# Gated attention, then hash-routed experts: identity products at the start, the multiplication by u a step later, the last group's turns in one piece, the last small block at the very end

## The chip, the cores and the metric

One NeuronCore of a Trainium2 chip runs the whole program. The metric is the device time of one execution in microseconds; the kernel before was run three times: 2505.44, 2507.41 and 2507.57, median 2507.41 us.

The engines by the names that the profile uses: PE is TensorE (matrix products; PEld its weight loads), DVE VectorE, ACT ScalarE, POOL GpSimd, SP SyncE, which here only issues DMAs. A "q" behind a name means the engine's queue that issues DMAs.

## The reference

```python
# attention: u, v are (8, 2496, 256), z is (8, 2496, 64), all float32
scores = (1.0 / S) * np.matmul(z, z.transpose(0, 2, 1))
attn = np.maximum(scores, 0.0) ** 2
x = u * np.matmul(attn, v)              # then reshaped to (19968, 256)
# experts: w1 is (8, 256, 1024), w2 is (8, 1024, 256)
expert_idx = token_ids * np.int64(2654435761) % np.int64(E)
for e in range(E):
    mask = expert_idx == e
    h = np.maximum(x[mask] @ w1[e], 0.0)
    out[mask] = h @ w2[e]
```

The score matrix is symmetric, and each token goes to exactly one expert, which its token id alone decides.

## The kernel before, in words

**Attention.** Each of the 8 batches is cut into 5 groups of queries (two stretches of up to 256, one of each half of the sequence) and 5 groups of keys. A step is one (batch, query group, key group), 200 in all, in the list `steps`; five steps with the same query group follow each other, and `pos` counts them 0 to 4. For a step, `score` (L212) makes the products of z (L228, tile `s_ps`) and ScalarE and VectorE turn them into squared positive scores `a` (L242 to L250). Scores below the diagonal are not computed: `mirror` (L267) transposes a finished tile, `keep` stores it in DRAM, and `recall` (L287) loads it back. `sums` (L256) forms four combinations `t` of the score quarters, `add_v` (L189) three of v, and `attend` (L297) multiplies in seven products instead of eight, a Strassen-like scheme, each of them accumulated over the five steps in half of a PSUM tile `acc` (L310). Four such tiles exist, and one group takes all four. After the fifth step `join` (L313) reads the seven sums and combines them into the output quarters `o`: ScalarE copies the first, VectorE does L322 to L328. The next group's first product overwrites what L322 reads, so it can only start behind it.

The main loop, from L773, runs ahead: in step i the scores and sums of step i + 2 are prepared, then `attend` of step i, then `join` at `pos` 4. The group's output is transposed on VectorE (`gate`, L331) and written to DRAM at `pos` 1 of the next group (`put`). At `pos` 3 `fetch` (L353) reads it back with tokens on partitions, as `x_row`, together with the rows of u (`u_sb`, L206). Five steps later, again at `pos` 3 and at the end of the step, `multiply` (L370, its operation on L374) multiplies `x_row` by u: four operations on VectorE. In this and the next step GpSimd scatters the rows to the slots of their tokens' experts (`sort`, L395, `x_slots` in DRAM).

While attention runs, `places` computes on VectorE and GpSimd which slot each token gets, `prepare` makes weight blocks with the sums that the seven-product scheme needs, and `enter` writes the token number of each slot.

**The last group** (batch 7, group 4) has no time for the way through DRAM. `gate_late` (L376) turns its output on TensorE instead (`transpose`, L384, into the PSUM tile `g_ps`), multiplies by u on VectorE (L386) and scatters. It is a generator that is advanced between parts of the first expert block. The group before it is fetched two steps before the end and multiplied at the end of the last step.

**Experts.** Sorted tokens are processed in 32 large blocks of 512 tokens and 35 small ones of 128. `load_x` reads rows from `x_slots`, `turn_x` transposes them on VectorE; for the first two blocks this is done inside the last two steps of attention (`turn_x_at_once`). `up_large` and `down_large` (L886, L917) make seven products each per part, in the order 1, 6, 7, 5, 2, 3, 4 that `products` (L860) writes out: VectorE's L866 adds the first two sums, L871, L872, L879 and L882 the rest, and `store` (L854, GpSimd) scatters finished rows to the output, four stores for a large block, one for a small. Products 1 and 5 go to PSUM tiles with the tag "held", in which later products are added; 6, 7 and 4 take tiles with the tag "other", of which `down_large` has one. `up_small` and `down_small` (L946, L962) are the plain two products of a small block.

The order of the work on TensorE is written out by hand in `ORDER` (L976): each letter advances one generator by a part. U and D are the large block's first and second product, u and d the small block's, X and x the transposition of rows for the next blocks, and G the generator `gate_late`. In the last round (i = 32) only D and d are left.

Of the kernel before, what the change touches and what calls it, by code (L numbers as in the profile page):

```python
# [11 lines left out]
F32 = mybir.dt.float32  # L12
# [13 lines left out]
def kernel(  # L26
# [10 lines left out]
    nc = tc.nc  # L37

    B, S, D = u.shape
    K = z.shape[-1]  # L40
    N = B * S
    E, _, F = moe_w1.shape
# [3 lines left out]
    P = 128  # L46
    L = 32
    DP = D // P
# [6 lines left out]
    NL = -(-(N - E * (BLK - 1)) // BLK)  # L55
# [9 lines left out]
    NT = -(-HS // (2 * P))  # L65
# [68 lines left out]
    ident = const.tile([P, P], F32)  # L134
# [8 lines left out]
    def keys(s, j):  # L143
        return P if (s, j) != (NT - 1, 1) else KL
# [225 lines left out]
    def multiply(b, g, x_sb):  # L370
        for q in range(2):
            for t in range(2):
                x, y = times_u(b, g, x_sb, q, t, keys(g, t))
                nc.vector.tensor_mul(x, x, y)  # L374

    def gate_late(b, g, o):  # L376

        x_sb = late.tile([P, 2, 2, D], F32, name="x_row")
        for q in range(2):
            ps = down_ps.tile([P, 2, D], F32, name="g_ps", tag="any")  # L380
            for t in range(2):
                m = keys(g, t)
                for i in range(DP):
                    nc.tensor.transpose(ps[0:m, t, ts(i, P)], o[:, i, q, ds(t * P, m)], ident[:])  # L384
                x, y = times_u(b, g, x_sb, q, t, m)
                nc.vector.tensor_mul(x, ps[0:m, t].rearrange("p (h i k) -> p i h k", h=DP, k=L), y)  # L386
                sort(b, g, x_sb, 2 * q + t)
            yield

    def sort(b, g, x_sb, k):  # L390

# [14 lines left out]
    SURE = 2  # L406
# [301 lines left out]
    def turn_x_at_once(j):  # L708
        for _ in turn_x(j):
            pass  # L710
# [17 lines left out]
    order = tc.manual_schedule()  # L728
    order.__enter__()

    for c in range(NZ):
        load_z(0, c, (nc.sync, nc.scalar) if c < 2 else None)
        if c < 2:
            turn_z(0, c)
        if c == 1:
            load_v(0, 0)
# [36 lines left out]
    for i, (b, g, s) in enumerate(steps):  # L773
# [11 lines left out]
        if pos == 0:  # L785
            acc = [acc_ps.tile([P, 2, W], F32, name="acc", tag="acc") for _ in range(4)]
        attend(b, g, s, ready.pop(i), acc, pos == 0, pos == NT - 1)
        if i >= len(steps) - SURE:
            turn_x_at_once(i - len(steps) + SURE)
        if pos == NT - 1:  # L790
            done = (b, g, join(g, acc, opool if i < len(steps) - 1 else late))
        prepare_mirror(i + AHEAD, a)
# [22 lines left out]
        if i >= 5 and not is_routed:  # L815
            is_routed = next(routed, True) is True
            if is_routed:

                rowpool = attention.enter_context(tc.tile_pool(name="rowpool", bufs=2))
        elif is_routed:  # L820
            if fetched and i >= fetched[0][0] + (5 if i < len(steps) - NT else 2):
                rows = fetched.pop(0)[1]
                multiply(*rows)
                to_sort += [(*rows, k) for k in range(4)]
            for _ in range(min(2, len(to_sort))):
                sort(*to_sort.pop(0))
            if len(fetched) < 2 and waiting and (len(waiting) > 1 or i > put_at + (1 if i < len(steps) - NT else 0)):
                fetched.append((i, fetch(*waiting.pop(0))))
# [133 lines left out]
    def down_small(j):  # L962
        ps = down_ps.tile([P, D], F32, name="o_ps", tag="any")
        for f in range(FP):
# [10 lines left out]

    ORDER = {"": "UuUDUuUDUdUDU" "XUDXUDUxUDUUDU", "made": "UuUDUuUDUdUDU" "XUDXuUDUxuUDUUDU",  # L976
             "next": "UuUDUuUDUdUDU" "XUDXUDUxUDUUxDU", "last": "UdUDUuUDUuUDU" "XUDXUDdUxUDUUDU",
             "first": "UUUUGUUGUUUUUUUU", "second": "DUDUUDUUDUUDUU" "xXUuDUXUuDUxUU"}

# [3 lines left out]
    def at(i):  # L985

        return [i, *SMALL[i]] if 0 <= i < NL else []

    for i in range(NL + 1):
# [10 lines left out]
        if i == 1:  # L1000
            parts["x"].insert(0, turn_x(SMALL[1][0]))
        parts = {p: chain(*x) for p, x in parts.items()}
        for p in ORDER["first" if i == 0 else "second" if i == 1 else next((k for k, n in (("made", i), ("next", i + 1), ("last", i - 1)) if len(at(n)) > 2), "")]:
            next(parts.get(p, iter(())), None)
        for p in parts.values():
            assert next(p, None) is None and next(p, "end") == "end"
# [45 lines left out]
```

## Time and profile before

The profiled execution took 2507.8 us; its span, from the first to the last instruction, is 2506.0 us, and the mean granted TensorE clock 0.998 of full speed.

| stage (us from the start) | length | PE busy | PE idle | DVE busy | share of DMA engines |
|---|---|---|---|---|---|
| 0 to 17.25: before the first product with v | 17.25 | 8.85 | 8.40 | 6.53 | 1.02 |
| 17.25 to 1453.9: the rest of attention | 1436.65 | 1430.68 | 5.97 | 1094.29 | 0.83 |
| 1453.9 to 1476: first expert block, last group's turns | 22.10 | 15.31 | 6.79 | 14.61 | 0.91 |
| 1476 to 2497.9: the experts | 1021.90 | 1021.54 | 0.36 | 537.52 | 0.68 |
| 2497.9 to 2506: behind the last product | 8.10 | 0 | 8.10 | 0.42 | 0.18 |

PE idle is length less PE busy. A share of the DMA engines above 1 means that transfers overlap on an engine. In the timeline's lines the columns are: start and duration in us, engine, line, operation, output<-inputs with shape, count of instructions merged into the row, and in brackets the idle time of the engine before it and what ended it. A line of the waits reads: engine, tile and line that waited <- what it waited for: us in total, times, longest. A line of the stretch tables: stretch, its length, busy time of the engine asked for, granted clock, DMA share, GB/s.

### The profile page before, as it was taken

How to read it: one execution, taken by the hardware profiler on the slowest of the kernel's cores; microseconds unless marked ns; L12 is line 12 of the kernel's file. 1: busy time of each engine (PE TensorE's matmuls, PEld its weight loads, DVE VectorE, ACT ScalarE, POOL GpSimd, SP SyncE). 2: the span in 40 equal slices, each digit the busy share in tenths (PEclk: the TensorE clock that was granted, in tenths of full speed). 3: DMA queues.
4: the chain of work that ended last, by engine and by line, in shares of the span. 5: the costliest groups of instructions: out<-in, count | busy, mean ns of one | idle time of the engine just before them, and what ended most of it. 6: DMA issues, size and time to landing. Idle time of an engine off the chain costs nothing.

```text
span 2506.0 us, 36968 instructions
## 1 busy us (share of the span) xinstructions
PE 2476.4 (99%) x13631; PEld 2110.9 (84%) x13631; DVE 1653.4 (66%) x3151; ACT 705.8 (28%) x1203; POOL 548.9 (22%) x532
## 2 busy tenths in 40 slices
PE   8999999999999999999999989999999999999998
PEld 6787787787787777877787889999999999999998
DVE  7798768768778677687687665545555555555553
ACT  4324324224223233133233112222222222222221
POOL 0000333322332233233223221111111111111112
PEclk9999999999999999999999999999999999999999
DMA  8776899798797897897888797766676667667762
GB/s 148 201 206 176 244 272 227 211 248 203 234 262 191 244 249 184 251 250 198 246 244 230 200 284 240 244 227 227 236 236 203 222 225 232 204 224 245 236 217 72
DMA packets 604661, 557.19 MB, mean 222 GB/s; under 512 B 287068, under 2 KB 544685, under 8 KB 594240
## 3 DMA queue, kind: packets, MB, share of 16 engines
q1 hardware_dynamic: 513984, 369.74, 54.6%
q10 hardware_dynamic: 63168, 97.86, 11.9%
q0 software_dynamic: 27328, 87.23, 10.0%
q8 instruction: 107, 1.75, 0.3%
q14 instruction: 74, 0.61, 0.1%
HBM read 375.55 MB, written 175.60 MB: 220 GB/s over the span
## 4 chain that ended last, share of the span: by engine, by line
PE 91%; DMA 5%; DVE 2%; issue 1%; SPq 0%; ACT 0%; POOL 0%; POOLq 0%; DVEq 0%; ACTq 0%
PE acc L310 42%; PE o_ps L931 16%; PE h_ps L901 15%; PE s_ps L228 8%; PE h_ps L954 5%; PE o_ps L965 5%; DMA a<-scores 3%; DMA u_sb<-in_u_dram 1%; DMA scores<-mirror 0%; DMA zn<-in_z_dram 0%; DVE x_row L374 0%; DVE t L261 0%; DVE t L262 0%; DVE t L263 0%; ACT a L242 0%
## 5 line engine op out<-in xcount | busy, mean ns | idle before, releaser
L242 ACT ACTIVATE a<-s_ps 128x512 f32<-128x512 f32 (+2 forms) x508 | 248.1, 579 | 736.5 <-PE s_ps L228 697.5
L310 PE MATMUL acc<-t,vc 128*128 128x256 f32 (+3 forms) x1600 | 402.6, 374 | 0.0
L310 PEld LDWEIGHTS acc<-a,v_sb 128*128 128x128 f32 (+1 forms) x1600 | 293.3, 190 | 125.0 <-issue 45.5
L310 PE MATMUL acc<-a,v_sb 128*128 128x256 f32 (+3 forms) x1600 | 382.6, 382 | 5.3 <-DVE o L322 5.2
L395 POOL DMA_INDIRECT x_slots<-x_row,row x160 | 192.3, 1202 | 849.7 <-DVE x_row L374 642.9
L310 PE MATMUL acc<-t,v_sb 128*128 128x256 f32 (+3 forms) x1600 | 369.7, 373 | 0.0
L310 PEld LDWEIGHTS acc<-t,vc 128*128 128x128 f32 (+1 forms) x1600 | 303.0, 190 | 34.5
L310 PEld LDWEIGHTS acc<-t,v_sb 128*128 128x128 f32 (+1 forms) x1600 | 303.5, 190 | 33.6
L261 DVE TENSOR_TENSOR t<-a 128x512 f32<-128x512 f32 (+1 forms) x200 | 134.5, 672 | 226.5 <-ACT a L250 162.0
L901 PE MATMUL h_ps<-xs,w 128*128 128x256 f32 x1024 | 258.1, 380 | 0.0
L931 PEld LDWEIGHTS o_ps<-w,h 128*128 128x128 f32 x2048 | 248.6, 192 | 6.5
L228 PE MATMUL s_ps<-zT 64*128 64x512 f32 (+1 forms) x960 | 241.4, 617 | 9.1 <-DVE zT L171 8.4
L931 PE MATMUL o_ps<-w,h 128*128 128x128 f32 x2048 | 249.3, 275 | 0.0
L908 ACT ACTIVATE h<-h 128x512 f32<-128x512 f32 x192 | 121.0, 630 | 349.1 <-DVE h L872 153.2
L854 POOL DMA_INDIRECT out_dram<-o_sb,idx x128 | 126.7, 990 | 420.8 <-ACT h L908 271.2
L272 DVE STREAM_TRANSPOSE mirror<-a 128x512 f32<-128x512 f32 x320 | 198.4, 677 | 6.6 <-DMA scores<-mirror 6.5
L310 PE MATMUL acc<-a,vc 128*128 128x256 f32 (+3 forms) x800 | 201.1, 374 | 0.0
L901 PE MATMUL h_ps<-xT,w 128*128 128x256 f32 x768 | 194.0, 382 | 1.2 <-DVE h L872 1.2
L901 PEld LDWEIGHTS h_ps<-xs,w 128*128 128x128 f32 x1024 | 178.5, 191 | 15.5
L931 PEld LDWEIGHTS o_ps<-w,hs 128*128 128x128 f32 x1536 | 186.4, 192 | 4.8
L931 PE MATMUL o_ps<-w,hs 128*128 128x128 f32 x1536 | 187.1, 275 | 0.0
L611 POOL DMA_INDIRECT slot_tokens<-token,addr x160 | 169.7, 1061 | 49.0 <-issue 48.1
(154 smaller groups left out, 2756.7 us busy)
## 6 DMA issues: line engine op xcount, KB each, us to landing
w<-w_blocks SPq DMA_DIRECT2D x64, 1792.0 KB, 11.3
scores<-mirror SPq DMA_DIRECT2D x276, 256.0 KB, 4.8
a<-scores ACTq DMA_DIRECT2D x48, 1024.0 KB, 5.8
w1s<-in_moe_w_dram SPq DMA_DIRECT2D x35, 1024.0 KB, 10.3
w2s<-in_moe_w_dram SPq DMA_DIRECT2D x35, 1024.0 KB, 11.5
a<-scores ACTq DMA_DIRECT2D x32, 896.0 KB, 7.3
w_blocks<-w POOLq DMA_DIRECT2D x16, 1792.0 KB, 8.1
u_sb<-in_u_dram SPq DMA_DIRECT2D x72, 256.0 KB, 5.2
```

Of the source, the lines that this page charges most:

```text
L228: nc.tensor.matmul(to, z_h[:, ds(h * HS + s * W + j * P, P)], at, start=True, stop=True)
L242: nc.scalar.activation(to, at, AF.Relu, scale=1.0 / S)
L261: nc.vector.tensor_sub(t1, y12, y11)
L272: nc.vector.transpose(m[:, :, j, h].rearrange("p (n i) k -> p i n k", i=QB), a[:, j, h].rearrange("p (i t) q r -> p i (t q) r", t=2))
L310: nc.tensor.matmul(acc[k][:, half, 0:w], x[0:n, j, :], y[0:n, j], start=(first and j == 0 and half == 0), stop=(last and j == 1), skip_gro ...
L395: st = nc.gpsimd.indirect_dma_start(out=x_dram[:, :], out_offset=bass.IndirectOffsetOnAxis(ap=row[0:m, c:c + 1], axis=0), in_=x_sb[0:m, q, ...
L611: st = nc.gpsimd.indirect_dma_start(out=slot_dram[:, None], out_offset=bass.IndirectOffsetOnAxis(ap=addr[0:n, to:to + 1], axis=0), in_=tok ...
L854: st = nc.gpsimd.indirect_dma_start(out=out[:], out_offset=bass.IndirectOffsetOnAxis(ap=idx[:, col:col + 1], axis=0), in_=o, in_offset=Non ...
L901: nc.tensor.matmul(ps[:, r], w1[j][:, k, ts(f + r, P)], y, start=first and r == 0, stop=True, skip_group_check=True)
L931: nc.tensor.matmul(ps[:, t], x[:, f, ts(t, P)], w2_block(w2[j], k)[:, f], start=first and t == 0 and f == 0, stop=f == FQ - 1, skip_group_ ...
L954: nc.tensor.matmul(ps[:, i, :], w1[j][:, c, ts(f + i, P)], x[:, 0, c, 0:P], start=(c == 0), stop=(c == DP - 1))
L965: nc.tensor.matmul(ps[:], hid[j][:, f], w2[j][:, f, :], start=(f == 0), stop=(f == FP - 1))
```

## The change

It has four parts.

- Twelve products of the identity with itself, into a PSUM tile of the score products' pool, are issued first on TensorE; nothing reads them.
- `multiply` comes six steps after `fetch` in place of five until the last ten steps of attention, five in the next five of them and two in the last five, as before; with six it falls at `pos` 4, behind `join`. For the last group but one it moves from the end of the last step to a place ahead of the last `join`. `turn_x_at_once` for the first two blocks runs one step earlier each.
- `gate_late` makes all eight transposes, into two tiles with the tag "held", in its first part, and all four multiplications and scatters in its second. In the first round's order the first G comes after four U's, as before, and the second after three more.
- In the last round the order is `DDDDDDDd`: all seven products of the large block, then the small block's. Before, the d stood between the second and the third D.

```diff
     def gate_late(b, g, o):
 
         x_sb = late.tile([P, 2, 2, D], F32, name="x_row")
+        made = []
         for q in range(2):
-            ps = down_ps.tile([P, 2, D], F32, name="g_ps", tag="any")
+            made.append(down_ps.tile([P, 2, D], F32, name="g_ps", tag="held", bufs=2))
+            for t in range(2):
+                for i in range(DP):
+                    nc.tensor.transpose(made[q][0:keys(g, t), t, ts(i, P)], o[:, i, q, ds(t * P, keys(g, t))], ident[:])
+        yield
+        for q in range(2):
             for t in range(2):
                 m = keys(g, t)
-                for i in range(DP):
-                    nc.tensor.transpose(ps[0:m, t, ts(i, P)], o[:, i, q, ds(t * P, m)], ident[:])
                 x, y = times_u(b, g, x_sb, q, t, m)
-                nc.vector.tensor_mul(x, ps[0:m, t].rearrange("p (h i k) -> p i h k", h=DP, k=L), y)
+                nc.vector.tensor_mul(x, made[q][0:m, t].rearrange("p (h i k) -> p i h k", h=DP, k=L), y)
                 sort(b, g, x_sb, 2 * q + t)
-            yield
+        yield
...
+    warm = mm_ps.tile([P, P], F32, name="warm", tag="mm")
+    for _ in range(12):
+        nc.tensor.matmul(warm[:], ident[:], ident[:], start=True, stop=True)
...
         attend(b, g, s, ready.pop(i), acc, pos == 0, pos == NT - 1)
-        if i >= len(steps) - SURE:
-            turn_x_at_once(i - len(steps) + SURE)
+        if 0 <= i - (len(steps) - 3) < SURE:
+            turn_x_at_once(i - (len(steps) - 3))
+        if i == len(steps) - 1:
+            multiply(*fetched[0][1])
         if pos == NT - 1:
             done = (b, g, join(g, acc, opool if i < len(steps) - 1 else late))
...
-            if fetched and i >= fetched[0][0] + (5 if i < len(steps) - NT else 2):
+            if fetched and i >= fetched[0][0] + (6 if i < len(steps) - 2 * NT else 5 if i < len(steps) - NT else 2):
                 rows = fetched.pop(0)[1]
-                multiply(*rows)
+                if i < len(steps) - 1:
+                    multiply(*rows)
                 to_sort += [(*rows, k) for k in range(4)]
...
-             "first": "UUUUGUUGUUUUUUUU", "second": "DUDUUDUUDUUDUU" "xXUuDUXUuDUxUU"}
+             "first": "UUUUGUUUGUUUUUUU", "end": "DDDDDDDd", "second": "DUDUUDUUDUUDUU" "xXUuDUXUuDUxUU"}
...
-        for p in ORDER["first" if i == 0 else "second" if i == 1 else next((k for k, n in (("made", i), ("next", i + 1), ("last", i - 1)) if len(at(n)) > 2), "")]:
+        for p in ORDER["first" if i == 0 else "second" if i == 1 else "end" if i == NL else next((k for k, n in (("made", i), ("next", i + 1), ("last", i - 1)) if len(at(n)) > 2), "")]:
```

## The prediction

> **What bounds the kernel now.** I read the busy table first, then TensorE's own waits, then its idle time cut by stage, and only then the timeline at each idle place.
>
> ```profile
> PE 2476.4 (99%) x13631; PEld 2110.9 (84%) x13631; DVE 1653.4 (66%) x3151; ACT 705.8 (28%) x1203; POOL 548.9 (22%) x532
> PE s_ps L228 <- DVE zT L171: 8.4, 2, 7.3
> PE g_ps L384 <- DVE x_row L386: 5.6, 2, 4.7
> PE acc L310 <- DVE o L322: 5.2, 7, 1.9
> ```
>
> TensorE (PE) is busy 2476.4 of 2506.0 us, so no reordering can gain more than the 29.6 us it is idle, unless its clock rises. Cut by stage, that idle time is 8.4 us up to 17.25 us, 6.0 in the rest of attention, 6.8 between 1453.9 and 1476, 0.4 in the experts and 8.1 after the last product. The change has one edit for each of the four large pieces.
>
> **Start: identity products.** Twelve 128x128 products of the identity are issued first on TensorE.
>
> ```profile
> 7.26 6.08 PE L228 MATMUL s_ps<-zT 64*128 64x512 f32 x16 [7.26 <-DVE zT L171]
> 13.38 1.77 DVE L171 STREAM_TRANSPOSE zT<-zn 128x736 f32<-128x736 f32 x2
> 14.47 2.78 PE L228 MATMUL s_ps<-zT 64*128 64x512 f32 x8 [1.14 <-DVE zT L171]
> ```
>
> A score product leaves two records here. Later four of them (eight records) take 1.92 us on the chain of waits, 0.48 each; here the pairs begin at 8.27, 9.12 and 9.98 us, 0.855 apart. So the array starts at nearly half speed although the granted-clock column prints 1.00, and four records take 1.92 us from 9.98 but 1.05 from 12.28: by then it is at full pace. The identity is ready at 1.38 us. An expert product of the same 128x128 shape leaves two records of 0.112 us pitch (sixteen L931 records, starts 1.79 us apart), so twelve last 2.7 us at full pace and 4.8 to 5.4 at the slow one: they end by 6.9, before 7.26, and can delay nothing. At full pace the first four score products end at 9.3 instead of 11.04; ScalarE's two pairs (1.08 us each) end at 10.6 instead of 12.16; the square L246 behind them (1.23) ends at 11.8 instead of 13.42; the third turn of z follows it. The fourth turn needs the last z transfer, issued at 9.49 and landing 3.2 to 4.0 us later, so 12.7 to 13.5. I take 13.0, plus 0.9 for the turn: 13.9 instead of 15.15. **Term 1.2 us**; 0 if the array is still slow at 7.26, 1.6 if the transfer is not last.
>
> The Trainium skill, page "TensorE: Matmul & The Clock Gate", Part 1, says the gate opens only after a free-running window of about 3.4 us was busy, and may shut after an idle one. The trace agrees as far as it goes: slow from 7.26 until some time between 10.8 and 12.3. By the page alone, a burst of about 5 us need not contain a whole window, so the term would be 0 or 1.2 at about even chance, an estimate from its window; the trace lets the gate open 3.6 to 5.0 us after the start, and I keep 1.2.
>
> **Attention: u a step later.** The four multiplications by u (L374, 1.43 us together) stand on VectorE ahead of the join of the group; the next group's products wait for the join's first read of the sums (L322).
>
> ```profile
> 884.63 1.66 DVE L374 TENSOR_TENSOR x_row<-x_row,u_sb 128x256 f32<-128x256 f32 x4 [1.84 <-DMA u_sb<-in_u_dram]
> 888.47 0.42 DVE L322 TENSOR_TENSOR o<-r,acc 128x256 f32<-128x256 f32 x1
> 888.94 1.78 PE L310 MATMUL acc<-a,v_sb 128*128 128x224 f32 x8 [0.89 <-DVE o L322]
> ```
>
> TensorE's timeline at the same place (third row) shows 0.89 us idle, released by L322. The other such gaps are 1.92 (at 379), 0.45 (560), 0.69 (707), 0.58 (741), 0.42 (1068) and 0.20 (1248). After the change the multiplication follows the join in VectorE's order, about 8 us later, one step. The same work stands in front of everything after it, and less in front of the join: at least 1.33 us, and 3.1 where u was late. Six gaps vanish (3.2 us); the one at 379 shrinks from 1.92 to 0.59. **Term 4.6 us**, from 3.2 (that one unchanged) to 5.2 (all). What waits for the multiplication is GpSimd's scatter L395 and, behind it in the same queue, the loads of weights L633 and the slot entries; GpSimd waits 642.9 us in 34 waits for x_row as it is, 19 each, with 22% of its time busy. The next fetch that needs a freed buffer of u comes four steps, 32 us, later. SyncE's order changes only in the first two batches. Moving `turn_x_at_once` a step forward changes no order on VectorE, since nothing else lies between: 0 both ways.
>
> **Transition: turns together.** Before, the third and fourth turns wait for VectorE to read the first two; the six rows show who is late.
>
> ```profile
> 1457.17 0.36 PEld L384 LDWEIGHTS g_ps<-ident,o 128*128 128x128 f32 x2
> 1457.74 0.43 DVE L374 TENSOR_TENSOR x_row<-x_row,u_sb 128x256 f32<-128x256 f32 x1 [0.56 <-DMA u_sb<-in_u_dram]
> 1458.81 1.10 DVE L374 TENSOR_TENSOR x_row<-x_row,u_sb 128x256 f32<-128x256 f32 x3 [0.64 <-DMA u_sb<-in_u_dram]
> 1462.48 0.51 PE L384 MATMUL g_ps<-ident,o 128*96 128x128 f32 x2 [4.71 <-DVE x_row L386]
> 1464.00:1466.00 2.00, 0.50 1.07 442
> 1474.21 1.13 PE L901 MATMUL h_ps<-xT,w 128*128 128x256 f32 x4 [1.18 <-DVE h L872]
> ```
>
> (The fifth is SyncE's stretch table: the granted clock was 0.50.) The change puts the multiplications of group 3 ahead of the last join. They wait for the same transfers of u, landing at 1457.7 and 1458.8, while the join used to run from 1454.64 to 1457.18. Now it runs from 1459.9 to 1462.4, and all eight turns wait for it: TensorE, done with its four first products at 1457.5, stands idle 4.9 us instead of 4.7 + 0.9. Then VectorE decides. At full clock: three additions 0.69 each to 64.5, product 3 to 65.4, product 4 to 66.3, L882 to 67.2, four multiplications (1.43) to 68.6, four sums (2.6) to 71.2, L866, L871, L872 to 73.4: TensorE resumes at 1473.45 instead of 1474.21, +0.76. If the clock drops again as it did, TensorE gives product 3 one microsecond later and it resumes at 1474.5, -0.3. **Term 0.2 us.** If u landed before the join were due, the join would end at 1458.7 and the same sum ends at 1470.0: +4.2. If u lands 2 us later, -2. The last scatters come some 3 us later (four at 1.28 after 67.5 or more, against the last at 1468.93); behind them on SyncE wait w1s L720 (1472.15), then the row loads xqs and xq (1472.92 to 1479.6), wanted by VectorE at 1493.6. With 8.6 us of landing xq is there at 1486, so 3 us are covered; beyond 7 they show.
>
> **End: the small block last.**
>
> ```profile
> 2485.33 3.62 PE L965 MATMUL o_ps<-w2s,h 128*128 128x256 f32 x16
> 2485.60 0.42 DVE L866 TENSOR_TENSOR ro<-ro,o_ps 128x256 f32<-128x256 f32 x1 [0.56 <-PE o_ps L931]
> 2501.15 0.97 POOL L854 DMA_INDIRECT out_dram<-o_sb,idx  x1 [0.30 <-issue]
> ```
>
> The small product (3.45 us pitch) moves from between products 6 and 7 to the end. It covered L866: product 7 writes the one "other" buffer that L866 reads until 2486.02, so TensorE now waits 2486.07 - 2485.33 = 0.74. It ends at 2498.6 instead of 2497.88. The large block's last two products end 3.45 - 0.74 = 2.7 sooner; its four stores follow at 1.275 each from 2494.6, so the fifth, the small block's, is issued at 2499.7 (its copy allows 2499.3) and done at 2500.7, against 2502.12. What follows the last store, 3.9 us, stays. **Term 1.4 us**; 2.2 without the bubble.
>
> **Sum.** 1.2 + 4.6 + 0.2 + 1.4 = 7.4 off the span of 2506.0: 2498.6. The profiled execution took 2507.8, 1.8 around its span, so 2500.4; the median of the runs shown lies 0.4 below it: **2500.0 us**. The terms' ends for this case alone (0 + 3.2 - 0.3 + 1.4 and 1.6 + 5.2 + 0.8 + 2.2) give 2503.1 to 2497.6.
>
> **Rivals.** *Turns pay in full*: upstream work is earlier and u with it, so the join is not held. 4 us more: 2496. For it: the transfers begin 6 us earlier in time. Against: so do the join and the recall that SyncE's queue waits for at 1428, so nothing moves relative to TensorE. *Given back*: the gaps return because the recalled scores, not the multiplications, are late; the start brings nothing. 1.7 + 0.2 + 1.4 = 3.3: 2504. For it: the chain goes through `DMA a<-scores` before most gaps, at 3.2% of the span. Against: at each gap the last releaser is L322, and L374 lies between the recall and it. *Slower by the new wait*: the multiplication now holds the last join, so each microsecond by which u lands later holds TensorE one for one. The longest landing of u anywhere is 11.9 us; from 1454.4 that is 1466.3, 7.5 later than now, and 1.7 more for a slow clock after the pause: 7.4 - 9.2, 2509. It decides from 5.7 us of lateness. For it: the transfers are queued at a share above 1 of the engines. Against: the median landing is 5.3.
>
> **Numbers.** Forecast 65%, in full 12%, given back 18%, slower 5%. A measurement of this kernel can tell about 0.2% from no change, 5 us: faster means below 2502.4. The forecast lies there nine times in ten, the first rival always, the second hardly: 0.73 faster, 0.23 same, 0.04 slower. The range, 2496.0 to 2504.6, takes in both middle rivals.
>
> **What would show it.** Right: second turn of z pair ended by 14; no acc gap over 0.6; multiplications ahead of the join ending near u's landing; a 0.7 us bubble ahead of product 7. Wrong: score products still 0.855 apart; gaps by L261 or recalls in place of L322; a longer pause before the turns.

## The result, and the profile after

The changed kernel took 2535.95 us (median of 6 runs, 2529.51 to 2539.14) against 2507.49 us of the kernel before (6 runs, 2505.44 to 2513.34): a ratio of 1.0105 (of the means, here and below), 95% interval 1.0087 to 1.0123. It is slower by 28 us, where 7.4 us less were forecast. The profiled execution took 2533.2 us, its span is 2531.4 us and its mean granted clock 0.993.

Line numbers of the changed kernel are higher than those of the kernel before: the scatter L395 is L399, the load of weights L633 is L637, their store L657 is L661, VectorE's sums of the experts L866, L872 and L879 are L878, L884 and L891, the expert products L901, L931 and L965 are L913, L943 and L977. L374, L310, L322, L261 are the same.

Cut at the same events, the two profiled spans differ above all in one stage:

| stage | before | after | difference |
|---|---|---|---|
| start to the first product with v | 17.18 | 16.11 | -1.07 |
| attention, to the first expert product | 1436.75 | 1461.96 | +25.21 |
| from there to the first second-layer product (the last group's turns) | 22.11 | 23.38 | +1.27 |
| from there to the end | 1029.99 | 1029.96 | -0.03 |

The last row holds a gain at the very end and, against it, most of a stretch at half clock behind the last group's turns.

First the busy times (the page's first part), then what TensorE waited for, both of the changed kernel:

```profile
PE 2494.3 (99%) x13655; PEld 2125.0 (84%) x13655; DVE 1652.4 (65%) x3151; ACT 706.4 (28%) x1203; POOL 533.5 (21%) x532
```

```profile
PE acc L310 <- DVE o L322: 10.3, 6, 4.2
PE s_ps L228 <- DMA zT<-zT: 4.6, 2, 3.4
...
PE acc L310 <- DMA a<-scores: 2.7, 1, 2.7
```

TensorE is busy 17.9 us more for 24 more records of work (4.9 us, the identity products), and idle 37.1 us where it was idle 29.6. The rest of the busy time, 13 us, is about what the clock takes, as the next lines show. Two of its drops, in the table of stretches (columns as in the prediction: stretch, length, busy time of TensorE, granted clock, share of the DMA engines, GB/s):

```profile
350.00:354.00 4.00, 4.00 (x13) 0.57 0.75 257
...
1115.00:1125.00 10.00, 8.79 (x18) 0.50 0.66 191
```

Between the first 15 us and the tail the kernel before had one stretch at half clock, of 3.4 us, behind the wait of 4.71 us for the last group's turns. The changed kernel has six of 3.4 us and one of 10.2, 30.7 us in all: half of that, 15.4 us, is lost, against 1.7. All but the one at 1487 us stand behind a pause of TensorE that the kernel before did not have, or had shorter. So the question is what made the pauses. VectorE's waits for the scores that are loaded back name most of it; first the changed kernel, then the kernel before:

```profile
DVE t L261 <- DMA a<-scores: 98.1, 20, 18.1
```

```profile
DVE t L261 <- DMA a<-scores: 52.7, 17, 12.0
```

VectorE waits 45 us more for recalls in total, and up to 18 us at once. Its timeline has such a wait at five of TensorE's six pauses of over 1.2 us in attention: 5.70, 8.42 and 7.94 us at 531, 898 and 1269, where the kernel before waits for no recall, and 18.15 and 13.80 us at 737 and 1113, where it waits 9.98 and 8.71. At the first three a wait of 3.3 to 4.0 us for the next batch's z rows follows, which the kernel before has too; at 1113 a late copy of z is the last to arrive. The first pause, 4.20 us at 346, is another matter: there VectorE waits 5.87 us for z rows, before 4.36, and for no recall. Nothing in the change touches a recall. GpSimd's own timeline shows what moved. The kernel before, at one group of batch 2 (the join is at 492.8; columns: start, duration, engine, line, operation, output<-input, count, idle time before and what ended it):

```profile
485.53 1.24 POOL L395 DMA_INDIRECT x_slots<-x_row,row  x1 [22.13 <-DMA scores<-mirror]
...
495.59 0.60 POOL L657 DMA_DIRECT2D w_blocks<-w  x1
...
523.88 1.10 POOL L395 DMA_INDIRECT x_slots<-x_row,row  x1 [24.73 <-DVE x_row L374]
...
527.99 0.78 POOL L633 DMA_DIRECT2D w<-in_moe_w_dram  x1
```

And the changed kernel, at the same group:

```profile
499.33 0.97 POOL L399 DMA_INDIRECT x_slots<-x_row,row  x1 [24.69 <-DVE x_row L374]
...
506.68 0.60 POOL L661 DMA_DIRECT2D w_blocks<-w  x1
...
511.41 0.78 POOL L637 DMA_DIRECT2D w<-in_moe_w_dram  x1
534.98 1.27 POOL L399 DMA_INDIRECT x_slots<-x_row,row  x1 [22.79 <-DVE x_row L374]
```

In both timelines GpSimd issues in the order of the program, and what waits for long there is the first scatter of a group, on the multiplication (the first row names a store of scores, but the first multiplication ended only 0.3 us ahead of it). Before, the load of the next weight block (1 MB) stood behind that scatter: 32.4 us after the store (1.8 MB) of the block before. Now the scatter is one step later in the program and the load is ahead of it: only three slot entries stand between store and load, so the load leaves 4.7 us behind the store. The store itself stands behind all four scatters, whose first now starts 3.3 us behind the join instead of 7.2 us ahead of it; the store moved from 2.8 us behind the join to 10.7. Three recalls, two of 0.9 MB and one of 1 MB, are issued at 10.1, 12.3 and 18.4 us behind the join of this group. So 2.8 MB of weights and 2.8 MB of scores, which used to follow one another, leave within 8.3 us. The second of these recalls, with its time from issue to landing in us at the end of the line, first in the changed kernel, then in the kernel before:

```profile
a<-scores ACTq DMA_DIRECT2D x1, 896.0 KB, 13.7
```

```profile
a<-scores ACTq DMA_DIRECT2D x1, 896.0 KB, 8.0
```

It lands at 522.06, and this is what follows from it in the changed kernel:

```profile
522.15 0.62 DVE L261 TENSOR_TENSOR t<-a 128x448 f32<-128x448 f32 x1 [5.70 <-DMA a<-scores]
...
528.50 0.94 DVE L171 STREAM_TRANSPOSE zT<-zn 64x736 f32<-64x736 f32 x1 [3.99 <-DMA zn<-in_z_dram]
...
532.06 1.21 PE L310 MATMUL acc<-a,v_sb 128*128 128x224 f32 x5 [1.31 <-DVE o L322]
```

In the kernel before VectorE does not wait for this recall, and TensorE has no pause at this join.

### The profile page after: what moved, and what is told of

It reads as the page before. It is cut to its first block, busy times and chain, and to the rows that moved or that the text cites. A ratio compares the mean times of both kernels' runs of the same rounds, so it can differ in the third digit from the quotient of the medians.

```text
span 2531.4 us, 36987 instructions
## 1 busy us (share of the span) xinstructions
PE 2494.3 (99%) x13655; PEld 2125.0 (84%) x13655; DVE 1652.4 (65%) x3151; ACT 706.4 (28%) x1203; POOL 533.5 (21%) x532
## 4 chain that ended last, share of the span: by engine, by line
PE 88%; DMA 7%; DVE 3%; issue 1%; SPq 1%; ACT 0%; POOL 0%; ACTq 0%; POOLq 0%; DVEq 0%
PE acc L310 40%; PE o_ps L943 15%; PE h_ps L913 15%; PE s_ps L228 8%; PE h_ps L966 5%; PE o_ps L977 5%; DMA a<-scores 3%; DMA v_sb<-in_v_dram 1%; DMA zn<-in_z_dram 1%; DMA scores<-mirror 1%; DMA u_sb<-in_u_dram 1%; DVE t L261 0%; DVE t L262 0%; SPq L281 0%; DVE t L263 0%
## 5 line engine op out<-in xcount | busy, mean ns | idle before, releaser
L310 PEld LDWEIGHTS acc<-a,v_sb 128*128 128x128 f32 (+1 forms) x1600 | 297.5, 192 | 134.5 <-issue 50.8
L310 PE MATMUL acc<-t,vc 128*128 128x256 f32 (+3 forms) x1600 | 404.7, 375 | 0.0
L310 PE MATMUL acc<-a,v_sb 128*128 128x256 f32 (+3 forms) x1600 | 389.2, 387 | 13.1 <-DVE o L322 10.3
L310 PE MATMUL acc<-t,v_sb 128*128 128x256 f32 (+3 forms) x1600 | 369.7, 374 | 0.0
L399 POOL DMA_INDIRECT x_slots<-x_row,row x160 | 174.0, 1088 | 888.3 <-DVE x_row L374 777.1
L310 PEld LDWEIGHTS acc<-t,vc 128*128 128x128 f32 (+1 forms) x1600 | 305.5, 191 | 34.6
L310 PEld LDWEIGHTS acc<-t,v_sb 128*128 128x128 f32 (+1 forms) x1600 | 303.5, 190 | 33.6
L261 DVE TENSOR_TENSOR t<-a 128x512 f32<-128x512 f32 (+1 forms) x200 | 134.5, 672 | 247.1 <-ACT a L250 142.2
L913 PE MATMUL h_ps<-xs,w 128*128 128x256 f32 x1024 | 258.6, 380 | 0.0
L943 PEld LDWEIGHTS o_ps<-w,h 128*128 128x128 f32 x2048 | 249.8, 193 | 7.3 <-DVE ro L878 0.8
L943 PE MATMUL o_ps<-w,h 128*128 128x128 f32 x2048 | 250.6, 276 | 0.6 <-DVE ro L878 0.6
L866 POOL DMA_INDIRECT out_dram<-o_sb,idx x128 | 126.4, 987 | 419.6 <-ACT h L920 251.2
L310 PE MATMUL acc<-a,vc 128*128 128x256 f32 (+3 forms) x800 | 201.6, 374 | 0.0
L913 PE MATMUL h_ps<-xT,w 128*128 128x256 f32 x768 | 193.0, 381 | 2.5 <-DVE h L884 2.5
L913 PEld LDWEIGHTS h_ps<-xs,w 128*128 128x128 f32 x1024 | 178.8, 191 | 15.6
L943 PEld LDWEIGHTS o_ps<-w,hs 128*128 128x128 f32 x1536 | 186.4, 192 | 4.8
L943 PE MATMUL o_ps<-w,hs 128*128 128x128 f32 x1536 | 187.1, 275 | 0.0
```

Source lines behind the costliest of these rows:

```text
L261: nc.vector.tensor_sub(t1, y12, y11)
L310: nc.tensor.matmul(acc[k][:, half, 0:w], x[0:n, j, :], y[0:n, j], start=(first and j == 0 and half == 0), stop=(last and j == 1), skip_gro ...
L399: st = nc.gpsimd.indirect_dma_start(out=x_dram[:, :], out_offset=bass.IndirectOffsetOnAxis(ap=row[0:m, c:c + 1], axis=0), in_=x_sb[0:m, q, ...
L866: st = nc.gpsimd.indirect_dma_start(out=out[:], out_offset=bass.IndirectOffsetOnAxis(ap=idx[:, col:col + 1], axis=0), in_=o, in_offset=Non ...
L913: nc.tensor.matmul(ps[:, r], w1[j][:, k, ts(f + r, P)], y, start=first and r == 0, stop=True, skip_group_check=True)
L943: nc.tensor.matmul(ps[:, t], x[:, f, ts(t, P)], w2_block(w2[j], k)[:, f], start=first and t == 0 and f == 0, stop=f == FQ - 1, skip_group_ ...
```

## The experiments

The theories, as they stood when the first traces had been read: the longer lag is the whole loss (A), or the earlier start and the held last join push the transfers together (B); and within A, a later scatter delays the recalls by itself (S), the multiplication behind the join delays VectorE (V), the order of GpSimd's queue does (Q, later C: store and load run into the recalls), or fetches that slip in the first batches do (A2). All times below are medians; each ratio is to runs of the kernel before on the same chip, with its 95% interval. The profiled stages of all kernels stand together behind the experiments.

**Which part of the change.** The lag alone, and everything but the lag:

```diff
# lag_alone, on the kernel before
-            if fetched and i >= fetched[0][0] + (5 if i < len(steps) - NT else 2):
+            if fetched and i >= fetched[0][0] + (6 if i < len(steps) - 2 * NT else 5 if i < len(steps) - NT else 2):
# all_but_lag, on the changed kernel: the same line the other way round
```

> The kernel before with one part of the change: multiply comes six steps after fetch. Theory A (the longer lag is the loss, alone): attention, from the first product with v to the first product of the experts, which grew from 1436.7 to 1462.0 us in the changed kernel, grows here by about as much: 2507.5 + 25 + some = 2530 to 2540, with several recall waits of over 7 us and five or more stretches of 3.4 us at half clock. Theory B (the transfers were pushed together by the earlier start, or the wait ahead of the last join spreads): 2500 to 2508, as the prediction's term of 4.6 us said.

Measured: 2538.07 us, ratio 1.0120 (1.0103 to 1.0137).

> The changed kernel with multiply five steps after fetch again: identity products, turns together, multiplications ahead of the last join and the end order stay. Theory A: attention is 1437 us again, start and end keep the 1.1 us that each showed, the transition costs its 0.85: 2507.5 - 1.4 = 2506 (2504 to 2508). Theory B: still 2520 or more.

Measured: 2508.68 us, ratio 1.0004 (0.9995 to 1.0014). Theory A holds and B falls: the lag is the whole loss. But the other three parts together bring nothing that can be told from zero, where the prediction had 2.8 us for them, which would lie outside the interval.

**Which steps.** The lag only from step 60 on, and only before it:

```diff
# lag_late
-  (6 if i < len(steps) - 2 * NT else 5 if i < len(steps) - NT else 2)
+  (6 if 60 <= i < len(steps) - 2 * NT else 5 if i < len(steps) - NT else 2)
# lag_early
+  (6 if i < 60 else 5 if i < len(steps) - NT else 2)
```

> The changed kernel with lag 6 only from step 60 on: fetches are at the steps they had before, and only the multiplications and scatters move by one step, to behind the join. Theory A1 (a scatter one step later is what delays the recalls, in every group): about 1462 * (140/200 of the loss): 2525 to 2532. Theory A2 (the loss comes of the fetches that slip in the first two batches, and of what that shifts): 2500 to 2507, with the acc gaps gone that the kernel before shows from 378 us on.

Measured: 2534.42 us, ratio 1.0107 (1.0090 to 1.0124): as much as the changed kernel, and a little more than A1 said.

> The changed kernel with lag 6 only before step 60, where it also moves seven fetches by one or two steps; from 60 on the multiplications stand ahead of the join as before. Theory A1: 2506 to 2512, since only the first quarter of the groups has the later scatter. Theory A2: 2525 to 2540, with late recalls spread over all batches.

Measured: 2514.57 us, ratio 1.0028 (1.0016 to 1.0041). This is above A1's range, but the steady state carries the loss: the lag in the first batches, slipped fetches and later multiplications together, costs some 6 us against all_but_lag where it stands alone, and nothing that shows where the rest of the lag is there too (lag_late against the changed kernel). Its mark is a pause of 4.59 us at 349 us with 6.8 us at half clock behind it; lag_late, with its fetches in their old steps, has no pause there.

**Which of the things that moved in the steady state.** Three kernels: the load back behind the scatters of the changed kernel; the load ahead of them in the kernel before; the scatters one step later in the program of the kernel before. (In the cuts below and further down, lines between the changed ones are left out.)

```diff
# load_behind, on the changed kernel
-        for part, after in enumerate((0, 4, 5, 7)):
+        for part, after in enumerate((1, 4, 5, 7)):
# load_early, on the kernel before
+        for part, after in enumerate((-1, 4, 5, 7)):
# scatter_later, on the kernel before
                 multiply(*rows)
-                to_sort += [(*rows, k) for k in range(4)]
+                later.append((i, rows))
+            if later and (i > later[0][0] or i >= len(steps) - 2 * NT):
+                _, rows = later.pop(0)
+                to_sort += [(*rows, k) for k in range(4)]
```

> The changed kernel, but the load of each weight block (prepare part 0, L637) is issued one step later, at pos 4, so that in GpSimd's queue it stands behind the first two scatters of the group again, as before the change; in the changed kernel it stands ahead of them, with only slot entries between it and the store of the block before. Theory Q (GpSimd's queue: the load is no longer held back by a scatter that waits for the multiplication, starts 4 to 6 us behind the 1.8 MB store instead of 26 to 33 us, and the two delay the recalls): the loss goes, 2500 to 2509, and store and load lie 25 us or more apart again. Theory S (the later scatters themselves delay the recalls) and theory V (the multiplication behind the join delays VectorE's sums): still 2525 or more.

Measured: 2528.25 us, ratio 1.0079 (1.0062 to 1.0096).

> The kernel before, with only the load of each weight block issued one step sooner, at pos 2, ahead of the scatters; multiplications and scatters stay where they were. Theory Q: 2525 to 2540, with late recalls and half-clock stretches as in the changed kernel. Theories S and V: 2505 to 2510.

Measured: 2518.80 us, ratio 1.0045 (1.0028 to 1.0062).

> The kernel before, multiplications where they were (pos 3, ahead of the join), scatters one step later (pos 4 and 0), so that GpSimd's queue has the changed kernel's order, load ahead of the scatters. Theories Q and S: 2525 to 2540. Theory V: 2505 to 2510.

Measured: 2515.36 us, ratio 1.0026 (1.0015 to 1.0038).

None of the three came out as a theory had it, so the order in the queue is not the whole of it. scatter_later did less than its name says: its scatters start where they did, the first 7.2 us ahead of the join of the group shown above in both kernels, behind a wait of 22 to 23 us. Only the load went ahead of them, as in load_early, so theory S has no test here. The times at which store and load were issued order the kernels better. Taken from the traces, in us behind the join, for groups 13 to 37:

| kernel | stores | loads | ratio |
|---|---|---|---|
| before | 2.8 to 7.8 | 0.3 to 1.4 (three at 33 to 36, just ahead of the next join) | 1 |
| scatter_later | 1.6 to 6.5 | 6.1 to 11.3 | 1.0026 |
| load_early | 2.8 to 7.8 | 6.0 to 11.2 | 1.0045 |
| load_behind | 10.7 to 16.3 | 6.9 to 11.1 | 1.0079 |
| lag_late | 10.7 to 16.7 | 15.4 to 21.3 | 1.0107 |

In the kernel before and in load_behind the load stands in the group after the store's, 26 to 38 us behind it; in the other three it follows the store within 3 to 6 us. load_behind put the load behind the scatter again, but the store stayed where the changed kernel had it, and most of the loss stayed too, though store and load were apart. So it is not their closeness alone. scatter_later and load_early, nearly equal in both columns, differ by less than their intervals. Theory Q became theory C: what counts is when the two leave, not what they stand behind.

**Store and load held at a fixed place.** A copy of one element on GpSimd, which reads what the join (or, in collide, the step's sums) wrote, holds the queue until then. lag_join is the changed kernel, before_join the kernel before, each with store and load at the group's end; collide is the kernel before with both in the middle of the group.

```diff
# lag_join and before_join, ahead of the scatters of the step
+        for part, after in ((0, 1), (3, 6)):
+            k, due = divmod(i - PREP - after, PERIOD)
+            if not due and 0 <= k < 2 * E:
+                nc.gpsimd.tensor_copy(tick[:], done[2][0:1, 0, 0, 0:1])
+                prepare(k, part)
-        for part, after in enumerate((0, 4, 5, 7)):
+        for part, after in ((1, 4), (2, 5)):
# collide, in the old place
+        for part, after in ((3, 9), (0, -1), (1, 4), (2, 5)):
+                if part in (0, 3):
...
+                    nc.gpsimd.tensor_copy(tick[:], ready[i + AHEAD][1][0:1, 0, 0, 0:1])
```

> The changed kernel with store and load of the weight blocks put back to where they ran before the change: both stand at pos 4 in GpSimd's queue, ahead of the scatters, behind a one-element copy of the join's output, so that they start when the group ends (before the change: store 3 to 8 us, load 1 us behind the join; in the changed kernel 11 to 17 and 15 to 21 us behind it, where the recalls are issued at 10.1, 12.3 and 18.4). Theory C (store and load run into the recalls; the longer lag does nothing else that costs): 2500 to 2508, no L261 wait over 13 us, and at most two stretches at half clock in attention. Theory S (the later scatters) or V (VectorE's order): 2520 or more.

Measured: 2519.17 us, ratio 1.0032 (1.0018 to 1.0047).

> Control for the former: the kernel before, store and load at the group's end in the same way, multiplications and scatters as before. Theory C: 2505 to 2509, and the former faster than this by the gaps ahead of the joins, 2 to 5 us. Theories S and V: the former slower than this by 15 us or more.

Measured: 2511.06 us, ratio 0.9998 (0.9988 to 1.0007); the kernel before took 2512.31 us in these runs.

> The kernel before, multiplications and scatters unmoved, but store and load issued one behind the other at pos 2, behind a one-element copy of that step's sums, some 10 to 15 us behind the join. Theory C: 2520 to 2540 with waits for recalls of over 13 us, like the changed kernel. Theories S and V: 2505 to 2510.

Measured: 2567.79 us, ratio 1.0220 (1.0199 to 1.0240). Its queue:

```profile
520.82 0.60 POOL L657 DMA_DIRECT2D w_blocks<-w  x1
521.42 0.17 POOL L837 COPY tick<-t 1x1 f32<-1x1 f32 x1
521.54 0.75 POOL L633 DMA_DIRECT2D w<-in_moe_w_dram  x1
```

The two leave 0.7 us apart, 18 to 24 us behind the join (later than I had meant), and the kernel loses 55 us, twice what the change lost, though no multiplication, scatter or fetch has moved in the program (by the trace the scatters start up to 11.4 us ahead of the join, before up to 8.6). So the place of store and load alone makes a loss of this kind, which is what theory C says, if not in this size. What waits was not what I expected. The waits for recalls stay at 49.5 us in total, longest 9.2; here the copies of z and the joins are late:

```profile
PE acc L310 <- DVE o L322: 19.5, 3, 8.1
PE s_ps L228 <- DMA zT<-zT: 11.3, 3, 6.5
```

The three late joins stand behind waits of VectorE of 9.38, 12.58 and 11.35 us for the next batch's z rows. So in these traces what is due behind the 2.8 MB is late, and the recalls are it only where they are due. lag_join shows the other direction: with the two transfers put back to the group's end, some 20 of the 28 us return (22 by the medians, 18 by the means). 7 to 8 us remain, and they are more than theory C allowed for; lag_join misses its expected range.

**What remains of the lag.** lag_join once more, with the lag only from step 60 on.

```diff
# lag_late_join, on lag_join
-  (6 if i < len(steps) - 2 * NT else 5 if i < len(steps) - NT else 2)
+  (6 if 60 <= i < len(steps) - 2 * NT else 5 if i < len(steps) - NT else 2)
```

> The changed kernel with store and load of the weight blocks at the group's end and lag 6 only from step 60 on, so that the fetches of the first two batches are at their old steps. Theory E (the 8 us left over are the slipped fetches, 3.5 us of pause and 3.4 of half clock at 350 us): no pause over 2.3 us around 350, ratio 0.998 to 1.001. Theory S (the later scatters and multiplications cost by themselves): ratio 1.002 or more, pauses near 568 and 1290 us as in the run with lag 6 throughout.

Measured: 2510.98 us, ratio 1.0020 (1.0010 to 1.0030): between the two theories. The pause at 350 us is gone; but the multiplication behind the join still brings none of the 4.6 us that were forecast. Its attention stage is 2.7 us longer than that of before_join, which alone is within the spread of such stages (below); the ratio is clear of noise. VectorE at 550 us, where the kernel before had a gap of 0.45 us:

```profile
549.89 0.62 DVE L261 TENSOR_TENSOR t<-a 128x448 f32<-128x448 f32 x1 [8.59 <-DMA a<-scores]
...
563.40 0.38 DVE L322 TENSOR_TENSOR o<-r,acc 128x224 f32<-128x224 f32 x1
```

No multiplication lies in front of this join any more. VectorE waits 8.59 us for a recall, then works without a pause for 13.5 us on what has piled up, and reaches the join 2.27 us too late. At 1283 us the same happens with a wait of 9.56 us and a gap of 2.61 us. This is the rival "given back", here with store and load out of the way. The lag makes these waits longer: in before_join, with store and load at the same place, the longest ones there are 4.24 us (at 541) and 3.19 us (at 1263). Whether the later scatters do it, or something else that the lag moved, these runs do not tell.

**The other three parts.** The turns alone, the start with and without more identity products, and the start with the end:

```diff
# warm_fill, on the kernel before: twelve identity products first, and behind the scores of the first two steps
+    spin(8)
# turns_alone, on the kernel before: gate_late, turn_x_at_once, the multiplication ahead of the last join, ORDER["first"]
# fill_all_but_lag: all_but_lag with spin(8) as above, spin(12) ahead of the last group's turns, spin(8) behind the first
# fill_end, on the kernel before: the order DDDDDDDd, spin(12) and spin(8) at the start, and in gate_late
+                if q == 0 and t == 0:
+                    spin(down_ps.tile([P, P], F32, name="warm2", tag="held", bufs=2), 18)
```

> The kernel before with only the last group's part of the change: all turns in one piece, multiplications ahead of the last join, the first blocks' turns a step earlier, the new first round. In the changed kernel and in the one with all but the lag, TensorE got from the first product of the experts to its third product 0.85 and 0.7 us later than before and lost 1.7 to 3.4 us to the clock. Theory P (this part costs, by the held join and the half clock behind it): 2508 to 2511. Theory of the prediction (+0.2): 2506.5 to 2508.

Measured: 2512.20 us, ratio 1.0005 (0.9992 to 1.0017; the kernel before took 2512.31 us in these runs), inconclusive between the two; in the trace the stage is 22.36 us against 22.11 of the kernel before.

> The kernel before with twelve identity products at the start and eight more behind the score products of the first two steps, where TensorE is idle from 11.1 to 12.7 us. In two of the five kernels with the twelve alone the clock fell to one half from 14.4 us on for 6.8 us. If the pause lets it fall: no stretch at half clock up to 25 us here, first product with v at 16.1 to 16.5, 2505.0 to 2506.5. If something else does, it still falls in some executions and the first product with v is at 18.

Measured: 2509.68 us, ratio 1.0012 (1.0002 to 1.0022). In its trace the first product with v is at 16.19 us and the clock does not fall before 1458 us, as expected; the time is not better for it, against the expectation.

> The changed kernel with lag 5, and more identity products where TensorE pauses: eight behind the score products of the first two steps, twelve ahead of the last group's turns, eight behind the first of them. Theory K (the clock falls behind these pauses and takes back what the three parts bring): no half clock before 25 us nor around the turns, start 1.0 and transition 1.7 to 3.4 us shorter than in the run without them: ratio 0.998 to 0.999. Against it: ratio 1.000 or above.

Measured: 2514.95 us, ratio 1.0034 (1.0021 to 1.0048), slower. The fault is in the experiment: the twelve products waited 5.77 us for the join's last operation (L328) instead of covering the wait, and the turns came behind them. The likely reason, which no run shows, is that their tile lies where the last sums of attention were. The run says nothing about the clock there; at the start the clock held, and the first product with v is at 16.38 us.

> The kernel before with the identity products at the start, eight more behind the first score products, eighteen in the 4.7 us pause ahead of the second pair of turns, and the new order of the last round; lag, turns and multiplications as before. Theory K: start 1.0, transition 1.7 (the 3.4 us at half clock), end 1.2: 3.9 us, ratio 0.9985. Against it: ratio 1.000, the recalls take back what comes sooner.

Measured: 2506.61 us, ratio 0.9994 (0.9985 to 1.0003). In the pause before the second pair of turns (first TensorE, then the stretch at the same place; before, 0.50):

```profile
1459.06 4.18 PE L738 MATMUL warm<-ident 128*128 128x128 f32 x36
1464.36 0.42 PE L384 MATMUL g_ps<-ident,o 128*96 128x128 f32 x2 [1.12 <-DVE x_row L388]
```

```profile
1462.00:1466.00 4.00, 2.88 (x21) 1.00 1.01 427
```

Each piece does about what theory K said, in its stage: 0.9 us at the start, 1.1 at the turns (1.7 expected), 1.3 at the end. Attention of this execution is 2.2 us longer and takes two thirds of it back. No version tried is faster than the kernel before by more than the measurement can tell.

The profiled stages, in us (the kernels that are unchanged in attention are the first seven):

| kernel | start | attention | turns | rest |
|---|---|---|---|---|
| before | 17.18 | 1436.75 | 22.11 | 1029.99 |
| before_join | 16.92 | 1440.81 | 22.63 | 1029.89 |
| warm_fill | 16.19 | 1434.90 | 22.93 | 1029.99 |
| turns_alone | 17.72 | 1440.48 | 22.36 | 1029.90 |
| all_but_lag | 18.22 | 1437.22 | 22.92 | 1028.57 |
| fill_all_but_lag | 16.38 | 1436.61 | 29.20 | 1028.72 |
| fill_end | 16.24 | 1438.98 | 21.02 | 1028.66 |
| after | 16.11 | 1461.96 | 23.38 | 1029.96 |
| lag_alone | 17.56 | 1468.19 | 22.09 | 1030.14 |
| lag_late | 16.45 | 1462.25 | 26.46 | 1028.75 |
| lag_early | 18.12 | 1441.74 | 23.17 | 1029.77 |
| lag_join | 18.31 | 1450.19 | 23.88 | 1029.04 |
| lag_late_join | 16.46 | 1443.49 | 23.73 | 1029.03 |
| load_behind | 16.09 | 1466.43 | 24.68 | 1028.49 |
| load_early | 16.87 | 1449.41 | 22.49 | 1030.31 |
| scatter_later | 17.27 | 1443.51 | 22.58 | 1030.14 |
| collide | 17.35 | 1495.45 | 22.59 | 1030.15 |

Among the first seven, attention lies between 1434.9 and 1440.8 us though its program is the same but for the weight transfers of before_join and the last steps of three of them: a spread of 6 us, larger than any of the three small terms.

## Why the prediction was wrong, point by point

**Attention: the step that failed.** "What waits for the multiplication is GpSimd's scatter L395 and, behind it in the same queue, the loads of weights L633 and the slot entries" was true of the kernel before and named the right queue. It was then costed at nothing, with "The next fetch that needs a freed buffer of u comes four steps, 32 us, later" as the only thing that could be late. The question asked was who is held back longer. The one to ask as well was who is no longer held back: one step later in the program the scatter stands behind the load, the load lost the wait that had kept it 26 to 33 us from the store, and the store, behind four scatters, came 5 to 11 us later. The term was +4.6 us; the stage lost 25.2. Of the 28 us, some 20 are the place of store and load (lag_join gives them back). For the fetches that slip there are 3 us (lag_late_join against lag_join, whose intervals overlap) and at most 6 (lag_early against all_but_lag, with the later multiplications of the first batches in it). The rest is not separated.

Two sentences beside it also failed. "The same work stands in front of everything after it" counted VectorE alone. And "SyncE's order changes only in the first two batches" was right, but no cost was put on it: there, at 346 us, the changed kernel has its first long pause, 4.20 us, with the slow clock behind it. SyncE issues the next z rows at 338.05 us, behind the slipped fetch, where the kernel before issued them at 332.05, ahead of it.

The six gaps were read from their last releaser, L322, with L374 in front of it. (The one at 707 us is 0.78 us in its row, not 0.69, so they add up to 3.3.) lag_late_join shows that reading to be half right: the gaps of 0.78, 0.89, 0.42 and 0.20 us are gone, that of 0.45 grew to 2.27 and that of 0.58 to 1.29, and new ones of 0.80 and 2.61 us stand at 924 and 1283 us. The rival "given back" had the evidence on its side, the chain's steps through the recalls, and 18%.

**No rival was on the right side of the loss.** The one slower rival had the wait for u at the last join, decided from 5.7 us of lateness. In the changed kernel u was late by little there:

```profile
1483.13 0.42 DVE L374 TENSOR_TENSOR x_row<-x_row,u_sb 128x256 f32<-128x256 f32 x1 [3.72 <-DMA u_sb<-in_u_dram]
```

That is 5.06 us behind the end of attention, against 3.81 before. The slower side lay in the transfers that the change moved without naming them.

**Start: mechanism right, range wrong at its lower end.** In the changed kernel the pairs of score products lie 0.43 to 0.53 us apart from the first on (0.855 before), and the first product with v came 1.07 us sooner, 1.2 forecast. But the range had 0 as its worst case. The work that comes sooner leaves TensorE a longer pause before the last transfers of z, and in three of the seven kernels with the twelve products alone (all_but_lag, lag_early, lag_join) the clock fell in it. lag_early, in stretches:

```profile
11.00:14.00 3.00, 1.87 (x5) 1.00 1.23 242
14.00:16.00 2.00, 1.60 (x5) 0.60 1.09 341
16.00:18.00 2.00, 2.00 (x4) 0.50 1.11 321
```

In these three the first product with v is at 18.1 to 18.3 us, in the other four at 16.1 to 16.5, in the kernels without identity products at 16.9 to 17.7: the term is about +1 or -1, by where the pause falls. That the one measured execution of the changed kernel shows +1.07 therefore owes something to luck. In the three kernels with eight more identity products in that pause it is at 16.2 to 16.4. The rule of the Trainium skill, page "TensorE: Matmul & The Clock Gate", Part 1, that the gate may shut after an idle window, was cited in the prediction for the burst and not asked about the pause behind it. In kind it agrees with the 0.50 from 14.4 us on; but the 3.41 us ahead of these three drops were idle for 1.47 to 1.90 us only.

**Turns: mechanism right, size missed, and small.** The forecast was an idle time of 4.9 us and +0.2 in all. The changed kernel shows 3.53 and 1.82 us, the join held by the multiplications as forecast, and 2.50 us of wait for VectorE behind it:

```profile
1485.22 0.33 PE L384 MATMUL g_ps<-ident,o 128*128 128x128 f32 x1 [3.53 <-DVE o L322]
1487.38 1.75 PE L384 MATMUL g_ps<-ident,o 128*128 128x128 f32 x7 [1.82 <-DVE o L328]
...
1499.20 1.13 PE L913 MATMUL h_ps<-xT,w 128*128 128x256 f32 x4 [2.50 <-DVE h L884]
```

TensorE resumes 21.13 us behind the first expert product instead of 20.28: -0.85, within the term's -2 to +4.2. The clock was at half again, as the variant at -0.3 had it, and u came 1.25 us later than before, which the prediction counted one for one. Behind the wait of 2.50 us the clock fell a second time, which the forecast did not have. Alone, in turns_alone, the stage is 0.25 us longer than before.

**End: right.** The bubble ahead of the seventh product is 0.58 us (0.74 forecast), the last store is issued 16.4 us behind the start of the sixth product (16.3 forecast), and from there to the end of the span it is 21.47 us instead of 22.63: 1.16 of the 1.4. All kernels with this order and a full clock after the turns end at 1028.5 to 1029.1 us in the last column against 1029.9 to 1030.3 without it.

```profile
2512.61 2.05 PE L943 MATMUL o_ps<-w,h 128*128 128x128 f32 x16 [0.58 <-DVE ro L878]
...
2521.65 3.62 PE L977 MATMUL o_ps<-w2s,h 128*128 128x256 f32 x16
```

## What to carry to other kernels

In a queue that is worked in order, a wait is also a brake for what stands behind it. When an instruction that waits is moved, list what it held back as well as what it will hold back, and look up what those transfers will meet at their new time. And where the gain to be had is a few us of pauses on the busiest engine, the same edit can put pauses of 2 us in other places, and most of these also cost clock.

## What the runs showed of the hardware

In these traces TensorE's granted clock falls to half for whole units of 3.41 us (stretches of 3.4, 6.8 and 10.2 us), and whether it does goes with TensorE's idle time in the unit before. I cut the 17 profiled executions into such units from the first drop of each, between 11 us and the last product. Of the units at full clock, all 48 with at least 2.0 us of idle time were followed by one at half clock; of 35 with 1.4 to 2.0 us, 13 were; of the more than 12000 with less, none. A unit that was itself at half clock was followed by another in 37 of 98 cases, in 13 of them with less than 0.5 us of idle time, so a drop can last longer than the pause explains. A pause can fall into two units: of the 30 pauses of 2 to 3 us behind the start, 21 had a drop within 3.4 us of their end, of 3.4 to 10.2 us, which costs up to half its length. The Trainium skill, page "TensorE: Matmul & The Clock Gate", Part 1, has the array go back to half speed after at least one idle window of about 3.4 us. The window's length is the one seen here, but it need not be idle: 2.0 us of it were always enough, and 1.47 us once.

The time at which a transfer is issued counted for much: the same 16 stores and 16 loads, 46 MB of the 557 MB that the program moves, made ratios of 0.9998 (before_join) and 1.0220 (collide) by their place within the group.
